# Half-column units, SBUF products and one shared PSUM tile in a long-convolution and gated-MLP kernel

## The chip, the cores and the metric

The kernel runs on one core of a Trainium2 chip. The metric is the device time of one execution in microseconds. Its engines are TensorE (PE, with its weight loads as PEld), VectorE (DVE), ScalarE (ACT), GpSimd (POOL, which here also issues the DMAs that store to scratch) and SyncE (SP, which issues all other DMAs). Matmul results land in PSUM, eight banks of 512 fp32 values in each of 128 partitions.

## The reference

With S = 2048 tokens, D = 640 columns, F = 1728 hidden units:

```python
xn = layernorm(A_q)                                   # no gain, no bias
k_shift = sum_t k[t - i] * shift_k[:, i], i = 0..3     # causal, four taps, by column
kv = k_shift * v
y = causal_conv(kv, ssm_k) + kv * ssm_D               # length S, by column (FFT of length 2S)
s = xn * y
g = silu(gelu_tanh(xn @ w1 + b1) @ w2 + b2)
out = A_q + s * g
```

All inputs and the output are bf16.

## The kernel before

The tokens lie as 128 partitions by 16 tiles `j` of 640 columns, so that the long convolution can be done as a transform of two steps with 64 x 32 points. D is added to the first tap of the kernel (`dadd`), so it needs no work of its own.

The work has these parts:
- **LN**: `stats`, `veps`, `pow` (POOL) and `xn`, for tiles in groups.
- **MLP**, in four chunks of four tiles: transposed `xn` (on PE for chunk 0, by DMA for the others), first layer `f1` (five matmuls of 512 columns for each of 14 hidden blocks, then a gelu on ACT), second layer `f2` (14 matmuls of 320 columns for each tile and column half, then silu). Chunks 2 and 3 go through `f1_wide`, which takes both into one two-bank tile and one gelu of 1024.
- **kv**: the four taps on DVE, six instructions per pair of tiles (L518 to L525).
- **Stage 1** (`s1_unit`, for the kernel `k` and for `u` = kv): for each tile two column halves, two matmuls each (L497), an eviction cast to SBUF on ACT or DVE (L234) and one store of 320 KB to scratch in DRAM (`scrK`, `scrU`; POOL, L501). The scratch turns partitions into the second transform's rows.
- **Convolution**, eleven units of three rows by 640 columns. A unit loads `kin` and `uin` (L586, SP), does stage 2 on PE (L596: eight matmuls side by side on 64 x 32 tiles of the array, four such packs a unit), casts the k result (L234), multiplies the u result straight from PSUM with it on DVE (L617, twice, 1920 products each: real and imaginary parts of one with both of the other), sums the four products in the first inverse step I1 on PE (L629, 32 matmuls, two of its four rounds with a third table), casts that (L234) and stores it to `scrC` (POOL, L638). It needs all 16 tiles of stage 1 for both k and u, with all columns.
- **End**: `cin` loads `scrC` (L644), I2 (L652) is the second inverse step, `ym` (L656, DVE) multiplies it from PSUM into `xn`, `f2m` (L470) does so with the MLP's result, `fin` (L448) adds x, and `store` (L450) writes the tile.

PSUM is four tiles of two banks. `G`, the second inverse table, is `W` transposed by 16 matmuls (L354) and one copy.

The order of all work is written out by hand: `ORDER` names for each operation its engine and its buffers, and `plan.emit` issues them in this order. Each engine, and each engine's DMA queue, works in order.

Of the kernel before, what the change touches and what calls it, by code (L numbers as in the profile page):

```python
# [32 lines left out]
NU = (NK1 + UK - 1) // UK  # L33
# [3 lines left out]
class Buf:  # L37
    def __init__(self, v=None, pool=None, parts=0):
        self.v, self.pool = v, pool
# [11 lines left out]
class Pool:  # L51
    def __init__(self, views, after=(), name=""):
        self.views, self.after, self.name = list(views), list(after), name
# [4 lines left out]
class Plan:  # L58
# [36 lines left out]
    def emit(self):  # L95
        seen = set()
        for i, e, slots in self.order:
            o = self.ops[i]
            assert o not in seen and all(d in seen for d in o.deps) and all(d in seen for d in o.after)
            for b, s in zip(o.allocs, slots):  # L100
                b.v = b.pool.views[s]
            o.fn(e)
            seen.add(o)
        assert len(seen) == len(self.ops)
# [13 lines left out]
1g 1g -2d 24d -6s 7d 1d -13s -1s -5a 13s -10s 17a 38d -54s 8s -4s 35d 1d -23a -20d -5g 30s 111p00 -112d -3p1 16d 7d  # L118
97p21 -10p32 -95d 9g 97a -104d 105p2 -137s 131d -5a -86d -23g 103p33 -70d -55g 143a -86d 70p2 -106a -14s 31g 88a 2a
-120s 4s 27d 19d 74p0 -86d -6d -6s 13p10 4p3 82a -85a 11d 1g -11p2 4p0 1d 7d -36s 39d -12a -2a 157d -70p1 -68p30 2p  # L120
2p2 2p 133d -115p0 116d -71a -49p1 -17a 62g 76d -178s 59p -29d 8a 11p3 -5a -13d 148d -128p -50s 61a -20a 3p2 -82d 217d
-133p 13a 3p 34g -45a 6a -8a -56s 197d 1d -146a 147d -145a 16a 130d -141p1 65p32 -11g 88d -76d -86s1 163d -162s 86p2
-66a 153d -171s 19p -20s 78p03 -57a 65a -140s 133a 201p3 -107d -86g -7p1 94d -93a 86p20 -207s 117g 92p0 -1a 7d 106p
-251p11 140a 6d -142p2 248a0 -169p02 75d -157a 84p3 -83p 82d -32g -46p 80a -83a 250d -246a 140d 12d -18g -136a 148p01
1d 1p3 -139p1 92s 40p03 2p2 6a -69g 62d 2a -133p 139g -79p30 2p0 -68p2 140g -135a -3p 5a 54p12 8a -150s 229d -81a -4p0
-62a 11p3 2p 247d -199a 87d -79g -24p11 18d -61a 10a 2a 244d -212a 211d -207p03 209d -252p2 44a -4p3 17g -12p1 -4a
-39p 44d 208d -158p00 -108p3 -91s 245d -141a -11p 108p1 -1a -94a -14a 165d -112g 70p02 -121a 123p2 -67g 42s 157p3
-147a 16a 28d 112g -182p11 40a 144d -182p2 -196a 276d 1d -108p03 26a 2a 180d -156g 147p -9p1 -189a 1p2 66g 143d
-191p00 180a1 -91d 108d -1d -352s 355d -9d -19p -188a 98p32 -80a 89d -81g 73a 116d -196p2 198d -46p0 -151a 80p3 19d
-256s 138g 107d 90d -105p21 116s0 -188g 99d 69a0 -88a 20d 89s -115p1 95d -88g 20d -260s 234a 76p 11p3 -69p13 -20a  # L130
15p20 109g -45a1 -63a 1p0 -282d 283a 72p -61d -26g -47p22 169d -103p0 -1a 76p1 31d -11s -26a0 -72g -61p3 72d 96d -103a
13p01 -79a 81p2 89d -29p 31s1 -88d -17g 18d -5a 6d -4a -80a -21p00 142d -36d -104p2 105d 1d 35p3 -41g -99a -2a 21g
-27p23 124d -122p0 147p -148a 8g 116d 72s -83p21 84s -39d -156a 163a1 -162g 112p0 10d -11a 2a 23p1 -42p22 87s 14s
-49a0 -32g 9d 24d -52a 29d -28p0 19p30 22p -20p2 -1a 9d 131s0 -159a 29p33 -28g 20d 10p0 3p21 7a0 -5p1 -14g 8a 2a 3d
64p310 -62a 124p02 -46p1 -82g 67a 16a -78g 85p3 2p1 38a 9s1 -46a 34s0 -55p2 19a 38d 2p0 1d0 1p1 -53p3 8p0 46d1 -61a
67s1 -59a 8a 52p23 2d -8p10 9p3 -7a 5d -6a 16s2 -6p2 -62p0 61d2 -60a 62d0 6s2 1p13 -6p20 7a 1d 1p1 -8a -73p3 74d 9p2
-81p0 80d1 7s0 -88a 83d0 -127d 133s3 1p13 12s4 -10d -1a -17g -77p2 104s1 -8p1 -91a 82p30 -86a 117s1 -21d2 1p2 1d0 -11a
18p31 -17a 20p0 -1a -8p12 7a -95p3 98d1 -8a -89a 98p2 -47g 53s2 -16d 18p01 11s0 -136p3 127a -9d0 -9g 28s0 -11a 2p1
21s1 -148a 118p20 2a 9p3 -10a 9d2 21s3 -12p01 2a -138p2 137a -8d0 10p1 -9p30 -129a 131a -1a -11g 41s4 -133p2 66g 46d1
1p0 8p13 -7d0 -113p 121d 1a -121a1 2p3 111p01 9p2 1d2 -122d 129s2 13s0 -29a -205d 194g 12a -112p 3p0 -2a1 120p1 8p23  # L140
2a -127p 118d0 8a -125a0 127p3 -9p12 -104p0 106a 9p2 -1d1 -9a 18p31 -140d 141a -123p 121s2 4p3 8s1 -18d0 9a -123a1
# [8 lines left out]
def kernel(  # L150
# [35 lines left out]
    smi = sb.tile([P, 256], F32, name="smi")  # L186
    pcol = sb.tile([P, 8], F32, name="pcol")
    pint = sb.tile([P, 8], I32, name="pint")
    tabs = sb.tile([P, 256], BF16, name="tabs")
# [5 lines left out]
    mv = sb.tile([P, NJ, nc.vector.BN_AGGR_DIM], F32, name="mv")  # L195
    veps = sb.tile([P, NJ], F32, name="veps")
# [6 lines left out]
    xnT = sb.tile([P, 2, DT, CH * P], BF16, name="xnT")  # L203
    hT = sb.tile([P, 2, FT, CH * P], BF16, name="hT")
    kT = sb.tile([P, NJ, D], BF16, name="kT")
    k_all = sb.tile([P, NJ + 3, D], BF16, name="k_all")
    v_all = sb.tile([P, NJ, D], BF16, name="v_all")
# [4 lines left out]
    def flat(t):  # L212
        return t[:].rearrange("p a d -> p (a d)")

    wb = mm[:, 0:4 * D].rearrange("p (a d) -> p a d", d=D)
    kt_t = mm[:, 4 * D:8 * D].rearrange("p (a b d) -> p a b d", a=2, d=D)
    kt_a = mm[:, 8 * D:10 * D].rearrange("p (a d) -> p a d", d=D)
    stg_t = [mm[:, (10 + 2 * i) * D:(12 + 2 * i) * D].rearrange("p (a d) -> p a d", d=D) for i in range(4)]
# [491 lines left out]
```

## Time and profile before

| | us |
|---|---|
| median of 3 runs (lowest to highest) | 216.5 (215.83 to 217.42) |
| profiled execution | 216.13 |
| its span, first to last instruction | 214.4 |
| PE, DVE, ACT busy | 179.4, 166.2, 126.5 |
| mean granted TensorE clock | 0.967 |

Busy time of an engine is the union of its instructions. The span leaves out the 1.73 us around the first and the last instruction. The first matmul of the MLP stands at 19.4 us, the first of the convolution at 102, and the last I1 ends at 180.6.

### The profile page before, as it was taken

Reading aid. Unit: us, or ns where it says so; the run is one execution under the profiler, and the core shown is the slowest. Engines: PE = TensorE matmul, PEld = TensorE weight load, DVE = VectorE, ACT = ScalarE, POOL = GpSimd, SP = SyncE. Lnnn points to the kernel's source line nnn. Section 1 sums busy time; section 2 is a strip of 40 time slices with the busy share of each in tenths; the row PEclk is TensorE's granted clock in tenths of the full one; section 3 lists DMA queues with packets and bytes.
Section 4 is the critical chain, followed back from the end, with each engine's and each line's share of the span. In section 5 each row is a group of like instructions: output and inputs, shape, how many; then the busy total and the mean of one; then the engine's idle time right before and its main releaser. Section 6 shows DMA issues by size and latency. Waiting matters only on the chain.

```text
span 214.4 us, 4137 instructions
## 1 busy us (share of the span) xinstructions
PE 179.4 (84%) x1660; PEld 90.4 (42%) x1660; DVE 166.2 (78%) x233; ACT 126.5 (59%) x163; POOL 37.6 (18%) x62
## 2 busy tenths in 40 slices
PE   0448999979988999998999899698999968999810
PEld 0314443633335665564443333233565523666500
DVE  6997998959889999964218997967756887029994
ACT  5298455877788977589554555868765764111100
POOL 7055000402252252324000020012100121100000
PEclk9999999999999999999999999999999995999985
DMA  5999998994379988949681749187980515599555
GB/s 165 373 418 412 413 356 203 361 387 172 144 214 369 242 247 206 255 151 343 214 276 27 250 144 303 27 272 257 292 278 6 199 49 192 160 415 409 207 199 198
DMA packets 28021, 52.54 MB, mean 245 GB/s; under 512 B 10081, under 2 KB 20834, under 8 KB 27874
## 3 DMA queue, kind: packets, MB, share of 16 engines
q1 hardware_dynamic: 23952, 35.89, 51.6%
q0 software_dynamic: 3904, 16.39, 20.3%
q8 instruction: 13, 0.21, 0.4%
q14 instruction: 6, 0.05, 0.1%
q10 hardware_dynamic: 146, 0.00, 0.0%
HBM read 31.95 MB, written 18.35 MB: 235 GB/s over the span
## 4 chain that ended last, share of the span: by engine, by line
PE 58%; DVE 20%; DMA 11%; issue 5%; ACT 3%; POOL 0%; DVEq 0%; ACTq 0%; POOLq 0%
PE ps L465 24%; PE ps L431 14%; PE ps L416 10%; DMA scrK<-mm 7%; DVE xn L656 5%; DVE k_all L617 5%; PE ps L629 4%; PE ps L596 3%; PE ps L497 3%; DMA x<-in_x_dram 2%; DVE stats L370 2%; DVE x L448 2%; DMA b_r<-in_b_dram 1%; DVE kT L448 1%; DVE mm L234 1%
## 5 line engine op out<-in xcount | busy, mean ns | idle before, releaser
L465 PE MATMUL ps<-w_sb,hT 128*128 128x320 bf16 x448 | 66.5, 303 | 1.4 <-ACT hT L420 0.8
L617 DVE TENSOR_TENSOR k_all<-ps,k_all 128x1920 bf16<-128x1920 f32 (+1 forms) x22 | 45.5, 2093 | 20.1 <-PE ps L596 17.1
L465 PEld LDWEIGHTS <-hT 128*128 128x128 bf16 x448 | 42.4, 99 | 24.5 <-issue 8.4
L234 ACT CAST mm<-ps 128x640 bf16<-128x640 f32 x55 | 35.1, 699 | 12.6 <-PE ps L497 6.9
L416 PE MATMUL ps<-xnT,w_sb 128*128 128x512 bf16 (+1 forms) x140 | 34.0, 393 | 1.9 <-ACT hT L420 1.6
L431 PE MATMUL ps<-xnT,w_sb 128*128 128x512 bf16 (+1 forms) x140 | 32.2, 380 | 0.6 <-ACT hT L439 0.5
L420 ACT ACTIVATE hT<-ps,b_f 128x512 bf16<-128x512 f32 (+1 forms) x28 | 18.2, 685 | 11.0 <-PE ps L416 11.0
L469 ACT ACTIVATE sl<-ps 128x640 bf16<-128x640 f32 x16 | 11.3, 707 | 21.5 <-PE ps L465 13.7
L439 ACT ACTIVATE hT<-ps,b_f 128x1024 bf16<-128x1024 f32 (+1 forms) x14 | 15.5, 1112 | 13.2 <-PE ps L431 13.1
L234 ACT CAST v_all<-ps 128x960 bf16<-128x960 f32 (+1 forms) x19 | 17.2, 947 | 9.0 <-PE ps L629 9.0
L416 PEld LDWEIGHTS <-w_sb 128*128 128x128 bf16 (+1 forms) x140 | 13.3, 101 | 20.0 <-issue 7.5
L638 POOL DMA_DIRECT2D scrC<-v_all x11 | 8.2, 749 | 73.0 <-ACT v_all L234 33.7
L431 PEld LDWEIGHTS <-w_sb 128*128 128x128 bf16 (+1 forms) x140 | 13.0, 98 | 18.0 <-issue 4.4
L234 ACT CAST k_all<-ps 128x960 bf16<-128x960 f32 (+1 forms) x16 | 14.2, 927 | 5.1 <-PE ps L596 4.1
L497 PE MATMUL ps<-kT,W 64*128 64x320 bf16 x64 | 8.9, 337 | 9.3 <-DMA kT<-in_kT_dram 8.3
L629 PE MATMUL ps<-k_all,tabs 32*64 32x480 bf16 (+1 forms) x352 | 13.3, 397 | 3.7 <-DVE k_all L617 1.9
L501 POOL DMA_DIRECT2D scrK<-mm x16 | 8.8, 550 | 42.8 <-ACT mm L234 35.3
L470 DVE TENSOR_TENSOR xn<-xn,sl 128x640 bf16<-128x640 bf16 x16 | 7.6, 484 | 9.9 <-ACT sl L469 9.9
L497 PEld LDWEIGHTS <-W 64*128 64x128 bf16 x128 | 4.8, 95 | 20.7 <-issue 11.6
L656 DVE TENSOR_TENSOR xn<-ps,xn 128x640 bf16<-128x640 f32 x16 | 12.6, 816 | 1.1 <-PE ps L652 1.1
L501 POOL DMA_DIRECT2D scrU<-mm x16 | 8.9, 556 | 19.0 <-ACT mm L234 14.7
L521 DVE TENSOR_TENSOR mm<-k_all,mm 128x2560 bf16<-128x2560 bf16 x8 | 11.9, 1490 | 0.2
(75 smaller groups left out, 176.7 us busy)
## 6 DMA issues: line engine op xcount, KB each, us to landing
scrK<-mm POOLq DMA_DIRECT2D x16, 320.0 KB, 6.6
scrU<-mm POOLq DMA_DIRECT2D x16, 320.0 KB, 3.3
k_all<-scrK SPq DMA_DIRECT2D x10, 480.0 KB, 3.9
v_all<-scrU SPq DMA_DIRECT2D x10, 480.0 KB, 4.7
scrC<-v_all POOLq DMA_DIRECT2D x10, 480.0 KB, 3.7
mm<-scrC SPq DMA_DIRECT2D x6, 640.0 KB, 6.4
kT<-in_kT_dram SPq DMA_DIRECT2D x4, 640.0 KB, 8.8
v_all<-in_v_dram SPq DMA_DIRECT2D x4, 640.0 KB, 7.1
```

Source lines behind the costliest of these rows:

```text
L234: (nc.scalar.copy if e == "ACT" else nc.vector.tensor_copy)(out=out_, in_=in_)
L416: nc.tensor.matmul(out=ps.v[0:M, i, :], lhsT=w1_sb[:, ft, t, 0:M], rhs=xnT_b[c].v[:, t, :], start=(t == 0), stop=(t == DT - 1))
L420: op("gelu", "ACT", lambda e, i=i, ft=ft, M=M: nc.scalar.activation(out=hT_b[c].v[0:M, ft, :], in_=ps.v[0:M, i, :], func=ACT.Gelu_apprx_ta ...
L431: nc.tensor.matmul(out=ps.v[0:M, i, :], lhsT=w1_sb[:, ft, t, 0:M], rhs=xnT_b[c + i].v[:, t, :], start=(t == 0), stop=(t == DT - 1))
L439: nc.scalar.activation(out=o, in_=s, func=ACT.Gelu_apprx_tanh, bias=b1_f[0:M, ft:ft + 1], scale=1.0)
L465: nc.tensor.matmul(out=ps.v[:, h, 0:H], lhsT=hT_b[c].v[0:M, ft, q * P:(q + 1) * P], rhs=w2_sb[0:M, ft, h * H:(h + 1) * H], start=(ft == 0) ...
L497: nc.tensor.matmul(out=ps.v[:, h, 0:H], lhsT=W[r, j, :], rhs=src[r, j, cs], start=True, stop=True)
L501: op("s1st" + kind, "POOL", lambda e: nc.gpsimd.dma_start(out=by_k1(scr)[:, 2 * j:2 * j + 2, :], in_=o.v), reads=[o], writes=[scr_b[j]], s ...
L521: op("kv2", "DVE", lambda e: tt(out=kt_t, in0=win(2, 2), in1=wbc(2, 2), op=ALU.mult), reads=kb + [wb_b], writes=[kvt_b])
L617: op("prod", "DVE", lambda e, ps=ps, qb=qb, kin=kin, w=w: nc.vector.tensor_tensor(out=qb.v[:, 0:4 * w].rearrange("p (i r w) -> p i r w", i ...
L629: nc.tensor.matmul(out=pc[g // 2].v[64 * r:64 * r + 64, g % 2, 0:w], lhsT=I1[tb][32 * g:32 * g + 32, :], rhs=qs[qi].v[32 * g:32 * g + 32, ...
L656: op("ym", "DVE", lambda e, j=j, ps=ps: nc.vector.tensor_tensor(out=hv(xn[:, j, :]), in0=ps.v[:, :, 0:H], in1=hv(xn[:, j, :]), op=ALU.mult ...
```

## The change

It does the following, with a new `ORDER` for all of it:
- k, v, the kernel and the three scratch arrays are laid out as two **column halves** `b` of 320. Stage 1 of u, kv and the convolution run by half; a kv step takes four tiles of one half, with the same instruction sizes as before. A store carries 160 KB in rows of 640 B; stage 1 of k makes two per tile.
- A convolution unit has six rows of one half (six units a half, the last of two rows) and is worked in **half units of three rows**. Stage 2 writes both parts of a half unit into one pair of banks, in two packs of eight matmuls of 240 columns (L638).
- Both the k and the **u result are cast** to SBUF (L259). The products are taken there in bf16, two instructions of 960 a half unit (L651), and **combined on DVE** into real and imaginary part, two instructions of 480 (L658, L659).
- **I1** (L669) then has two rounds instead of four: 16 matmuls a unit.
- `inv_unit` does I2 and `ym` for two tiles of one half (L691, L698), so a tile's `fin` waits for both halves and the MLP.
- PSUM is **one tile of eight banks**, given out by bank (`f1`, `f2`, `xt`) or by pair. `f1_wide` is gone; each gelu takes 512 and each silu 320 columns.
- `G` comes from four DMA transposes on SP (L386). Ten matmuls on zeros (`warm`, L300) are added. One tile's statistics are taken on ACT (L400). POOL may do `f2m` and `fin`. The small tables are built with fewer instructions.

```diff
-    ps_t = [psum.tile([P, 2, 512], F32, name="ps%d" % i) for i in range(4)]
+    ps_t = psum.tile([P, 8, 512], F32, name="ps")
...
-    op("gtr", "PE", gtr, reads=[W_b, id_b], writes=[ps])
...
+    for i in range(CH):
+        op("gtr", "SP", lambda e, i=i: nc.sync.dma_start_transpose(
+            out=G[:, 4 * i:4 * i + 4, :], in_=W[:, 4 * i:4 * i + 4, :].rearrange("p a b -> p (a b)")), reads=[W_b], mods=[G_b],
+           size=128 * 1024)
...
+        for t in range(nh):
+            for nm, src in (("s2k", kin), ("s2u", uin)):
+                ps = pair()
+
+                def s2(e, src=src, ps=ps, t=t):
+                    for i in range(2):
+                        for r in range(2):
+                            for g in range(4):
+                                nc.tensor.matmul(out=ps.v[32 * g:32 * g + 32, r, i * w:(i + 1) * w],
+                                                 lhsT=F2[i][64 * r:64 * r + 64, :],
+                                                 rhs=part(src.v[64 * r:64 * r + 64], t)[:, g * w:(g + 1) * w], start=True, stop=True)
+
+                chain("s2", op(nm, "PE", s2, reads=[src[t], tab_b], writes=[ps], extra=last("s2")))
+                op("s2ev", "ACT|DVE", lambda e, src=src, ps=ps, t=t: evict(
+                    e, part(src.v, t).rearrange("p (r c) -> p r c", r=2), ps.v[:, :, 0:2 * w]), reads=[ps], writes=[src[t]],
+                   size=4 * w)
+
+            def prod(e, t=t):
+                q = qb.v[:, t * 8 * w:(t + 1) * 8 * w].rearrange("p (r i m c) -> p r i m c", r=2, i=2, m=2)
+                ku, uu = (part(x.v, t).rearrange("p (r i c) -> p r i c", r=2, i=2) for x in (kin, uin))
+                for r in range(2):
+                    nc.vector.tensor_tensor(out=q[:, r], in0=uu[:, r, :, None, :].to_broadcast([P, 2, 2, w]),
+                                            in1=ku[:, r, None, :, :].to_broadcast([P, 2, 2, w]), op=ALU.mult)
...
+            def comb(e, t=t):
+                q = qb.v[:, t * 8 * w:(t + 1) * 8 * w].rearrange("p (r i m c) -> p r i m c", r=2, i=2, m=2)
+                nc.vector.tensor_tensor(out=q[:, :, 0, 0], in0=q[:, :, 0, 0], in1=q[:, :, 1, 1], op=ALU.subtract)
+                nc.vector.tensor_tensor(out=q[:, :, 1, 0], in0=q[:, :, 1, 0], in1=q[:, :, 0, 1], op=ALU.add)
...
+            for i in range(2):
+                for r in range(2):
+                    for g in range(4):
+                        nc.tensor.matmul(out=pc[g // 2].v[64 * r:64 * r + 64, g % 2, 0:nh * w].rearrange("p (t c) -> p t c", t=nh),
+                                         lhsT=I1[i][32 * g:32 * g + 32, :], rhs=q[32 * g:32 * g + 32, :, r, i, 0, :],
+                                         start=(i == 0), stop=(i == 1))
...
+    for b in range(2):
+        for u in range(NU):
+            conv_unit(b, u)
```

Three places of the order. On **DVE** where the products begin, the queue before has all kv steps (`mm`, `v_all`) behind it, then casts (L234) and products (L617):

```order
L523 TENSOR_TENSOR mm<-mm 128x1280
L525 TENSOR_TENSOR v_all<-mm,v_all 128x1280
L234 CAST mm<-ps_99 128x2x320 x2
L234 CAST k_all<-ps_97 128x960
L617 TENSOR_TENSOR k_all<-ps_97,k_all 128x1920
L617 TENSOR_TENSOR k_all<-ps_98,k_all 128x1920
L234 CAST k_all<-ps_100 128x960
```

In the changed kernel the first unit's products (L651) and combinations stand between a kv step of half 1 (L554), the normalization of later tiles (L425) and the statistics of the last ones (L415):

```order
L554 TENSOR_TENSOR mm<-mm 128x1280
L425 TENSOR_SCALAR xn<-kT,mv,rstd 128x640 x2
L497 TENSOR_TENSOR xn<-xn,sl_97 128x640
L651 TENSOR_TENSOR k_all<-v_all,xtra 128x960 x2
L658 TENSOR_TENSOR k_all<-k_all 128x2x240
L659 TENSOR_TENSOR k_all<-k_all 128x2x240
L651 TENSOR_TENSOR k_all<-v_all,xtra 128x960 x2
L658 TENSOR_TENSOR k_all<-k_all 128x2x240
L659 TENSOR_TENSOR k_all<-k_all 128x2x240
L415 BN_STATS stats<-kT 128x6 x2
```

The products have moved ahead of two kv instructions, two statistics, five normalizations and the second half's last stage-1 casts.

On **DVE** at the end, the queue before alternates `ym` (L656) and `fin` (L448) to the last row:

```order
L656 TENSOR_TENSOR xn<-ps_99,xn 128x640
L470 TENSOR_TENSOR xn<-xn,sl_95 128x640
L448 TENSOR_TENSOR kT<-xn,kT 128x640 x3
L448 TENSOR_TENSOR x_85<-xn,x_85 128x640 x2
L656 TENSOR_TENSOR xn<-ps_98,xn 128x640
L448 TENSOR_TENSOR x_85<-xn,x_85 128x640
L656 TENSOR_TENSOR xn<-ps_100,xn 128x640
L448 TENSOR_TENSOR x_85<-xn,x_85 128x640
```

In the changed kernel the eight `ym` of half 0 (L698) follow the last cast of the convolution, and the queue ends with the MLP's product (L497) and `fin` (L473):

```order
L473 TENSOR_TENSOR x_86<-xn,x_86 128x640
L497 TENSOR_TENSOR xn<-xn,sl_97 128x640
L473 TENSOR_TENSOR kT<-xn,kT 128x640 x2
L698 TENSOR_TENSOR xn<-ps,xn 128x2x320
L473 TENSOR_TENSOR kT<-xn,kT 128x640
L497 TENSOR_TENSOR xn<-xn,sl_98 128x640
L473 TENSOR_TENSOR kT<-xn,kT 128x640
```

What comes last has moved from I2 and `ym` to the second layer of the MLP.

On **SP** where the convolution's loads begin, the queue before holds only loads of `scrK` and `scrU` (L586), after all transposes of `xn`:

```order
L586 DMA k_all<-scrK 128x3x640 x2
L586 DMA v_all<-scrU 128x3x640
L586 DMA k_all<-scrK 128x3x640
L586 DMA v_all<-scrU 128x3x640 x2
L586 DMA k_all<-scrK 128x3x640 x2
```

In the changed kernel the loads (L621) alternate with the transposes of `G` (L386) and of the third and fourth chunk's `xn` (L450):

```order
L386 DMA_TRANSPOSE G<-W 128x4x128
L621 DMA k_all<-scrK 128x6x320
L621 DMA v_all<-scrU 128x6x320
L450 DMA_TRANSPOSE xnT<-xn 128x5x128
L386 DMA_TRANSPOSE G<-W 128x4x128
L621 DMA k_all<-scrK 128x6x320
L621 DMA v_all<-scrU 128x6x320
L450 DMA_TRANSPOSE xnT<-xn 128x5x128 x2
L621 DMA xtra<-scrK 128x6x320
```

The second unit's loads have moved behind one transpose of `xn` and one of `G`.

On PE the new order, counted in matmuls, is: first layer of chunk 0 (70, with stage 1 between), second layer of chunk 0 (112), first layer of chunk 1 (70), the first stage-2 operation (16), second layer of chunk 1, in which the first I1 stands behind four of its eight groups, and from there chunks 2 and 3 with the rest of the convolution between them. Behind the last I1 stand 140 matmuls of the second layer and 64 of I2; before there were 112 and 64.

More of the change, by code (lines that the diff above doesn't have):

```diff
@@ L100, in emit @@
             for b, s in zip(o.allocs, slots):
[L101 removed]
+                b.v = b.pool.view(s, b.width)
             o.fn(e)
@@ L202 @@
     w2_sb = sb.tile([P, FT, D], BF16, name="w2_sb")
[L203 to L207, printed above, removed]
+    xnT = sb.tile([P, 2, DT, CH * P], BF16)
+    hT = sb.tile([P, 2, FT, CH * P], BF16)
+    kT = sb.tile([P, 2, NJ, H], BF16, name="kT")
+    k_all = sb.tile([P, 2, NJ + 3, H], BF16, name="k_all")
@@ L263 @@
     op("first", "DVE", c0, writes=[bias_b, mh_b])
+    op("zero", "DVE", lambda e: nc.vector.memset(xtra[:, 0:D], 0.0), writes=[z_b])
+    for _ in range(10):
+        ps = bank()
+        op("warm", "PE", lambda e, ps=ps: nc.tensor.matmul(out=ps.v[:], lhsT=xtra[:, 0:P], rhs=xtra[:, P:P + 512], start=True, stop=True),
+           reads=[z_b], writes=[ps])
     def iotas(e):
@@ new lines, in conv_unit, with inv_unit, mmy, ym @@
+            op("i1ev", "ACT|DVE", back, reads=[pc[i]], mods=[uin], size=2 * nh * w)
+        op("cst", "POOL", lambda e: nc.gpsimd.dma_start(out=by_n2(scrC)[:, b, k0:k1, :],
+                                                        in_=uin.v[:, 0:n].rearrange("p (k d) -> p k d", d=H)),
+           reads=[uin], writes=[scrC_b[b][u]], size=P * n * 2)
+    def inv_unit(b, i, cb):
+        j = 2 * i
+        ps = pair()
+        def mmy(e):
+            for t in range(2):
+                for h in range(2):
+                    nc.tensor.matmul(out=ps.v[64 * h:64 * h + 64, t, 0:H], lhsT=G[:, j + t, 64 * h:64 * h + 64],
+                                     rhs=cb.v[:, h, j % 4 + t, :], start=True, stop=True)
+        op("i2", "PE", mmy, reads=[cb, G_b], writes=[ps])
+        def ym(e):
+            xv = xn[:, j:j + 2, b * H:(b + 1) * H]
+            nc.vector.tensor_tensor(out=xv, in0=ps.v[:, :, 0:H], in1=xv, op=ALU.mult)
+        op("ym", "DVE", ym, reads=[ps], mods=[xn_b[j], xn_b[j + 1]])
+        step_done(j)
+        step_done(j + 1)
```

508 lines of the change are left out of this document (245 added, 263 removed).

## The prediction

> **What bounds the kernel now.** First the window view, cut at four points of the chain: the first matmul of the MLP (19.4), the first matmul of the convolution (102), the end of its last I1 (180.6), the end. Above it the sums of the page's first part.
>
> ```profile
> PE 179.4 (84%) x1660; PEld 90.4 (42%) x1660; DVE 166.2 (78%) x233; ACT 126.5 (59%) x163; POOL 37.6 (18%) x62
> ```
>
> ```profile
> core 0: us, PE busy (x) PEld busy (x) DVE busy (x) ACT busy (x) POOL busy (x), PEclk, DMA share, GB/s
> 0.00:19.40 19.40, 7.41 (x52) 4.53 (x53) 16.04 (x43) 11.81 (x14) 8.99 (x19) 1.00 0.89 335
> 19.40:102.00 82.60, 78.40 (x494) 38.97 (x502) 72.18 (x118) 61.45 (x92) 20.34 (x33) 1.00 0.85 275
> 102.00:180.60 78.60, 71.05 (x947) 32.56 (x948) 56.67 (x36) 49.69 (x53) 6.97 (x10) 0.97 0.57 186
> 180.60:214.40 33.80, 22.56 (x176) 14.39 (x176) 21.34 (x37) 3.50 (x5) 1.26 (x2) 0.85 0.69 258
> ```
>
> In the second stage PE is busy 95% and DVE 87%; in the third PE 90% (71.05 of 78.6), DVE 72%, ACT 63%; in the last nobody is full, because it is a sequence: the scratch round trip, then DVE. Each stage follows the other, and DVE's slack lies in the third and the last. The chain that ended last shows the same and gives what PE work costs in a row:
>
> ```profile
> 19.43 15.99 PE ps L416 x65
> ...
> 69.67 2.06 PE ps L465 x14
> 71.73 0.38 PE ps L497 x4
> 72.11 2.01 PE ps L465 x14
> ...
> 101.98 0.53 PE ps L596 x16
> 102.52 8.96 PE ps L431 x40
> ...
> 123.72 1.02 PE ps L629 x32
> 124.74 0.33 PE ps L596 x8
> ...
> 180.58 10.86 PE ps L465 x70
> 191.44 0.41 PE ps L652 x4
> ...
> 211.09 0.49 DVE x L448
> ```
>
> So an MLP matmul of 512 columns costs 0.224 us (8.96/40), a second-layer group of 14 costs 2.01, four stage-1 matmuls 0.38. Stage 2 comes in packs of eight that run side by side: sixteen take 0.53, eight 0.33, so a pack of 480 columns is 0.20 and the rest, about 0.13 to 0.2, is paid per excursion. An I1 of 32 is four packs, 0.95 to 1.02. After the last I1, at 180.58, come 33.8 us: PE fills 10.86 with second-layer groups while scrC is written and read, then DVE alone works from 191.9 to 211.6, then the last store takes 2.8 (214.4 less 211.58).
>
> **The change, part by part.** The durations:
>
> ```profile
> L617 DVE TENSOR_TENSOR k_all<-ps,k_all 128x1920 bf16<-128x1920 f32 x20 | 42.6, 2154 | 19.6 <-PE ps L596 17.1 <-issue 1.3 <-ACT v_all L234 0.7
> L234 ACT CAST v_all<-ps 128x960 bf16<-128x960 f32 x18 | 16.5, 961 | 8.5 <-PE ps L629 8.5
> L521 DVE TENSOR_TENSOR mm<-k_all,mm 128x2560 bf16<-128x2560 bf16 x8 | 11.9, 1490 | 0.2
> L469 ACT ACTIVATE sl<-ps 128x640 bf16<-128x640 f32 x16 | 11.3, 707 | 21.5 <-PE ps L465 13.7 <-DVE xn L656 6.3 <-DVE xn L470 1.3
> L470 DVE TENSOR_TENSOR xn<-xn,sl 128x640 bf16<-128x640 bf16 x16 | 7.6, 484 | 9.9 <-ACT sl L469 9.9
> L234 DVE CAST mm<-ps 128x640 bf16<-128x640 f32 x9 | 7.4, 824 | 5.7 <-PE ps L497 3.0 <-DMA scrK<-mm 2.3 <-issue 0.5
> L234 DVE CAST k_all<-ps 128x960 bf16<-128x960 f32 x6 | 6.8, 1152 | 3.2 <-PE ps L596 2.2 <-issue 1.0
> L656 DVE TENSOR_TENSOR xn<-ps,xn 128x640 bf16<-128x640 f32 x16 | 12.6, 816 | 1.1 <-PE ps L652 1.1
> L420 ACT ACTIVATE hT<-ps,b_f 128x512 bf16<-128x512 f32 x26 | 17.0, 686 | 11.0 <-PE ps L416 11.0
> L439 ACT ACTIVATE hT<-ps,b_f 128x1024 bf16<-128x1024 f32 x13 | 14.5, 1112 | 10.8 <-PE ps L431 10.6
> ```
>
> *Products (DVE).* Removed: 22 products straight from PSUM, 45.6 us (42.6 and two shorter ones). Added: 40 products of 960 elements and 4 of 640, and 40 combinations of 480 and 4 of 320, all in SBUF. Between the rows of 640 (484 ns) and 2560 (1490) an SBUF product costs 0.524 ns an element and 149 fixed. Hence 652 for 960, 484 for 640, 400 for 480, 317 for 320: 28.0 + 17.3 = 45.3. The products move no DVE time; twice the rate is spent on the combinations. No row shows a product whose both inputs repeat along a middle dimension; L521 has one such input. The bounds are 652 ns and one element per PSUM rate, (2154 - 154)/1920 = 1.04 ns, that is 1.15 us; I take 652, the nearest shape.
>
> *Evictions.* The u results, until now read from PSUM by the product, must now be cast: 22 more of about 960 elements. By the new order DVE makes 20 conv casts (16 of 960, 2 of 640, 2 of 320: 21.1 us by 1152, 824 and an estimate of 0.49, 824 less 320 at 1.04) instead of 9 (10.0), ACT 48 (44.5 us by 961) instead of 35 (31.4). DVE also makes 3 more stage-1 casts (+2.5) and gives POOL four 640-element operations (-1.9). So DVE goes from 166 to about 177 us in sum and ACT, with unpaired gelus (56 x 0.686 = 38.4 against 17.0 + 14.5 and 2.5 for the last, shorter ones) and halved silus (32 x 0.44, an estimate: 707 less 320 x 0.83, the slope between L420 and L439), from 126 to about 146.
>
> *PE.* I1 halves: ten of two packs (0.53) and two short ones (0.27) are 5.8 us against 10.5, a gain of 4.7. The sixteen transposes of W leave PE (1.9). Stage 2 has twice the matmuls at half the columns: 44 operations of two packs of 240. Between a pack cost proportional to its columns (0.10) and one that stays at 0.20 lie 8.8 us; I take 0.10, since the start of a matmul on another tile of the array costs next to nothing in these rows:
>
> ```profile
> L596 PE MATMUL ps<-v_all,tabs 64*32 64x320 bf16 x16 | 0.7, 305 | 0.5 <-ACT k_all L234 0.3 <-ACT v_all L234 0.2
> 174.87 0.33 PE L596 MATMUL ps<-v_all,tabs 64*32 64x320 bf16 x8 [0.22 <-ACT v_all L234]
> ```
>
> Eight matmuls of 305 ns each are over in 0.33 us, so seven starts lie within 25 ns, some 4 ns apart.
> The Trainium skill, "TensorE: Matmul & The Clock Gate", section "Wait — 56ns, not 53.3ns?", says instead that start-to-start never drops below about 25 ns however few columns there are. By that rule sixteen matmuls need 0.40 us whatever their width, stage 2 costs 8.8 us more, and that is the fourth rival below. The trace speaks against it for matmuls on different tiles of the array, and the same page's section "The mechanism" also gives about 4 ns there.
>
> *Scratch and queues.* The rows of scrK, scrU and scrC become 640 B instead of 1280 to 2560, and POOL issues 64 stage-1 stores of 160 KB instead of 32 of 320. The bytes are the same; DMA is at 0.57 in the third stage. POOL, 37.6 us busy, has room for some 20 us of issues. What counts is the latency:
>
> ```profile
> scrU<-mm POOLq DMA_DIRECT2D x16, 320.0 KB, 3.3
> k_all<-scrK SPq DMA_DIRECT2D x10, 480.0 KB, 3.9
> v_all<-scrU SPq DMA_DIRECT2D x10, 480.0 KB, 4.7
> scrC<-v_all POOLq DMA_DIRECT2D x10, 480.0 KB, 3.7
> mm<-scrC SPq DMA_DIRECT2D x6, 640.0 KB, 6.4
> ```
>
> The four transposes of G move to SP, where two stand ahead of the second unit's loads; until 94 us DVE has no room for that unit, so that is the cover. Ten warming matmuls lie in PE's idle time before 19.4, two between stage-1 groups (0.2 each).
>
> *When the convolution begins.* Half 0 needs only the first half's u. In PE's new queue 140 first-layer matmuls (31.4), ten second-layer groups (20.1), 88 stage-1 matmuls (22 x 0.38 = 8.4) and one stage-2 operation stand ahead of the first s2u: 60 us after 19.4, that is 80, against 102 now with all u behind it. The last u store and its reload (0.7 + 0.6 + 3.3 + 4.7 after the last stage-1 group of half 0, ten us of PE work earlier at 70) land at 80 as well. But DVE is later. To 102 us it now spends 16.04 + 72.18 = 88.2 us; of that the new order puts behind the first product two kv steps, two statistics, five normalizations, two casts and one MLP product, and ACT takes one statistic: about 9 us. That leaves 79. With 16 of it done at 19.4, and 90% busy after (87% now), the first product starts at 19.4 + 63/0.9 = 90, and the first unit's combinations end at 94.3 (4.2 us of DVE). PE's I1 of that unit stands behind two second-layer groups, so PE arrives at about 85.5 and waits nine us: everything queued behind it, the next s2 and the MLP, waits too.
>
> *From there to the last I1.* DVE has left: 20 half units of 2.1 us (40.8 with the two short ones), casts 21.0, stage-1 casts 4.1, two statistics 2.3, five normalizations 2.2, five MLP products 2.4, kv 1.6: 74.4, less about 3.4 for consecutive operations that overlap (the x16 of L656 fill 12.6, not 13.1): 71. PE has 140 first-layer matmuls 31.4, ten groups 20.1, sixteen stage-1 matmuls 1.5, 40 stage-2 operations 8.0 and 17 excursions 3.4, I1 5.8: 70.2. ACT has about 75 from 77 on. The two bounds are equal; the present third stage ran its one bound engine at 90%, so with two I take 87%: 71/0.87 = 81.6, and the last I1 ends at 176 instead of 180.6.
>
> *The tail.* Behind it PE has ten second-layer groups, 20.1, and sixteen I2 (0.27 for four matmuls plus 0.14 a switch from the 0.41 row, seven switches), 5.3: 25.4. Half 1's first I2 stands 10.4 us down that queue; cast, store and reload (0.5 + 0.8 + 3.2 + 6.4) take 10.9, so 0.5 to 0.7 of waiting. DVE's rest is sixteen L656 (12.6), fourteen final adds and four MLP products (18 x 0.42), 20 us, and lies beside PE's 25.4, because half 0's eight are done before half 1 arrives. Then silu 0.44, product 0.48, add 0.48, gaps 0.15, store 2.8: 4.35. Together 30.4 against 33.8.
>
> **The sum.** 176 + 30.4 = 206.4 us of span, 8 less than 214.4. The profiled execution took 216.13, 1.73 more than its span, and 0.4 less than the median of 216.5. So 208.1, rounded **208**: 3.9% faster. The gain is two parts of about 4: the stages overlap, and the DVE-only tail becomes a PE tail.
>
> **Rivals.**
> 1. *The queues feed each other better*: DVE is busy 95% of the stretch, near what it reaches now in the middle of the second stage:
>
> ```profile
> 60.00:90.00 30.00, 28.62 (x212) 16.69 (x210) 29.32 (x48) 23.33 (x36) 10.82 (x15) 1.00 0.93 263
> ```
>
>    Last I1 at 169, time 201. Against it: PE must then be busy 94% too.
> 2. *In-order waits eat the gain.* Each of the twelve I1 waits in PE's queue for combinations that wait for casts that wait for that PE. L617 idled 17.1 us for L596 in this way. A loss of 0.9 us a unit more than I took (77% busy) puts the last I1 at 186.5 and the time at 219. From 0.7 us a unit the gain is gone.
> 3. *Slower: SBUF products at one element per cycle.* Place: L651 and its two combinations. Price 0.52 ns on 61,400 elements, 32 us, all on the engine that bounds: 100 us at 92% after a first unit of 7, last I1 at 206, time 238. It decides from 0.83 us a product of 960 (8 us over 44). For it: two repeated inputs and strides that no row shows; against it: L521.
> 4. *A half-length pack costs a full one*: 8 us more on PE after the first I1; 78.2 at 90% is 87 us, last I1 at 181.5, time 214. It is the mechanism to which the 25 ns rule would lead.
>
> **Chances.** Forecast 0.50 (203 to 213), first rival 0.13, second 0.20 (215 to 223), third 0.07, fourth 0.10. To leave out two in ten at most, the range runs from 199 to 219: it takes in the forecast, the first, the fourth and about half of the second. Less than 1% is about what a measurement of this kernel tells from no change. Faster by more: 0.48 + 0.13 + half of the fourth, 0.66; within: 0.02 + 0.08 + 0.05 = 0.15; slower: 0.12 + 0.07 = 0.19.
>
> **What would show it.** L651 at 0.65 us and L658 at 0.40 (third rival: 1.15). First L651 at about 90, and a PE wait of several us at the first L669. Sixteen L638 matmuls in about 0.3 to 0.4 us (fourth: 0.53). DVE busy near 177, ACT near 146. Last I1 at 176, and from there PE, not DVE, on the chain to within 5 us of the end. I am wrong if the first product waits for scrU beyond 95, if DVE is under 80% busy from 94 to the last I1, or if half 1's I2 waits for its reload more than 2 us.

## The result

| | before | changed |
|---|---|---|
| median, lowest to highest | 216.45 us (215.83 to 217.42, 4 runs) | 205.25 us (203.5 to 209.48, 4 runs) |
| profiled execution, its span | 216.13, 214.4 | 204.61, 202.4 |
| PE, DVE, ACT busy | 179.4, 166.2, 126.5 | 175.4, 172.3, 138.4 |

The ratio is **0.945** (95% interval 0.937 to 0.953), faster by 5.5%. The forecast was 208 in a range of 199 to 219. Executions of the changed kernel scatter more than those of before; ratios, and the means given below, leave out executions that ran markedly slower than the fastest ones of the same kernel, so they can differ from the medians.

The windows of the changed kernel, cut at the first matmul of the MLP, the first I1, the end of the last I1 and the end. The columns are as in the prediction. The first I1 is not the event at which the kernel before was cut: 102 was its first matmul of stage 2, and its first I1 stood at 116.9. Here the first matmul of stage 2 stands at 86.4; the last two rows are cut there.

```profile
0.00:19.40 19.40, 7.97 (x39) 3.52 (x40) 14.37 (x39) 9.39 (x13) 8.10 (x24) 1.00 0.92 337
19.40:97.90 78.50, 69.98 (x486) 33.73 (x485) 69.07 (x107) 58.07 (x94) 38.91 (x54) 1.00 0.91 280
97.90:173.00 75.10, 72.59 (x1131) 35.05 (x1130) 67.77 (x123) 64.22 (x88) 18.38 (x23) 0.98 0.89 249
173.00:202.40 29.40, 24.88 (x211) 16.18 (x204) 21.10 (x35) 6.67 (x13) 5.20 (x4) 0.99 0.64 202
19.40:86.40 67.00, 58.86 (x342) 27.16 (x339) 59.40 (x84) 46.88 (x77) 34.05 (x47) 1.00 0.89 288
86.40:173.00 86.60, 83.71 (x1266) 41.63 (x1266) 77.45 (x144) 75.41 (x105) 23.24 (x30) 0.98 0.91 246
```

The difference between length and PE's busy time is PE's idle time. Before it was 12.0, 4.2, 7.6 and 11.2 us in the four stages, 35.0 in all; now, with stage 2 as the cut in both, it is 11.4, 8.1, 2.9 and 4.5, together 27.0. The 12 us of span that went are thus **8 us of PE idle time and 4 us of PE's busy time** (179.4 to 175.4, although 4.9 of warming matmuls are new). The idle time went in the tail (-6.7) and in the convolution (-4.7). The second stage has 3.9 more, although it is 16 us shorter.

The convolution's end and the tail, from the chain that ended last:

```profile
172.75 0.28 PE ps L669 x16
173.02 2.01 PE ps L491 x14
175.03 0.94 PE ps L691 x12
...
193.96 3.93 PE ps L491 x28
197.93 0.04 issue
197.98 0.45 ACT sl L495
198.45 0.50 DVE xn L497
198.97 0.49 DVE kT L473
```

From 173 to 197.9 the chain is PE alone (and from 115 on with but 3 us of ACT between); before, DVE followed DVE from 191.9 on. And the groups that answer to those of before:

```profile
L651 DVE TENSOR_TENSOR k_all<-v_all,xtra 128x960 bf16<-128x960 bf16 x16 | 9.7, 652 | 0.3
L659 DVE TENSOR_TENSOR kT<-kT 128x480 bf16<-128x480 bf16 x8 | 3.2, 399 | 0.0
L669 PE MATMUL ps<-k_all,tabs 32*64 32x480 bf16 (+1 forms) x128 | 4.4, 339 | 0.0
L669 PE MATMUL ps<-kT,tabs 32*64 32x480 bf16 x64 | 2.8, 421 | 0.0
```

I1 never waits (idle before it 0.0); its sum is 7.2 us.

### The profile page after: what moved, and what is told of

It reads as the page before. It is cut to its first block, busy times and chain, and to the rows that moved or that the text cites. A ratio compares the mean times of both kernels' runs of the same rounds, so it can differ in the third digit from the quotient of the medians.

```text
span 202.4 us, 4736 instructions
## 1 busy us (share of the span) xinstructions
PE 175.4 (87%) x1846; PEld 88.5 (44%) x1846; DVE 172.3 (85%) x301; ACT 138.4 (68%) x206; POOL 70.6 (35%) x103
## 4 chain that ended last, share of the span: by engine, by line
PE 47%; issue 17%; DMA 13%; POOL 13%; DVE 5%; ACT 3%; SPq 1%; POOLq 0%; ACTq 0%; DVEq 0%
PE ps L459 18%; PE ps L491 18%; DMA scrU<-mm 9%; POOL scrK L532 6%; POOL scrU L532 4%; PE ps L638 4%; DMA x<-in_x_dram 3%; PE ps L669 3%; PE ps L691 3%; ACT mm L259 2%; POOL rstd L422 2%; DVE mm L259 1%; DVE stats L415 1%; PE ps L524 1%; ACT L495 1%
## 5 line engine op out<-in xcount | busy, mean ns | idle before, releaser
L459 PE MATMUL ps<-xnT,w_sb 128*128 128x512 bf16 (+1 forms) x280 | 68.9, 392 | 4.7 <-ACT mm L259 3.5
L259 ACT CAST mm<-ps 128x640 bf16<-128x640 f32 x52 | 34.2, 698 | 23.1 <-PE ps L524 11.2
L459 PEld LDWEIGHTS <-w_sb 128*128 128x128 bf16 (+1 forms) x280 | 25.6, 100 | 41.5 <-issue 17.1
L463 ACT ACTIVATE hT<-ps,b_f 128x512 bf16<-128x512 f32 (+1 forms) x56 | 36.7, 697 | 8.1 <-PE ps L459 8.0
L532 POOL DMA_DIRECT2D scrU<-mm x32 | 22.3, 753 | 42.7 <-ACT mm L259 37.5
L259 ACT CAST v_all<-ps 128x960 bf16<-128x960 f32 (+2 forms) x34 | 30.3, 928 | 3.8 <-PE ps L669 2.3
L495 ACT ACTIVATE sl<-ps 128x320 bf16<-128x320 f32 x32 | 14.1, 445 | 21.5 <-PE ps L491 21.2
L532 POOL DMA_DIRECT2D scrK<-mm x32 | 23.4, 903 | 5.7 <-ACT mm L259 5.3
L524 PEld LDWEIGHTS <-W 64*128 64x128 bf16 x128 | 5.3, 97 | 25.9 <-issue 19.4
L698 DVE TENSOR_TENSOR xn<-ps,xn 128x640 bf16<-128x640 f32 x16 | 12.5, 816 | 4.1 <-PE ps L691 4.0
L259 DVE CAST v_all<-ps 128x960 bf16<-128x960 f32 (+2 forms) x12 | 12.2, 1014 | 4.3 <-PE ps L669 2.2
L259 DVE CAST mm<-ps 128x640 bf16<-128x640 f32 x12 | 9.6, 817 | 6.8 <-PE ps L524 5.9
L553 DVE TENSOR_TENSOR mm<-k_all,mm 128x2560 bf16<-128x2560 bf16 x8 | 11.9, 1485 | 0.2
L550 DVE TENSOR_TENSOR mm<-k_all,mm 128x2560 bf16<-128x2560 bf16 x8 | 11.9, 1486 | 0.1
L638 PEld LDWEIGHTS <-tabs 64*32 64x32 bf16 x704 | 7.6, 90 | 9.5 <-issue 8.4
L651 DVE TENSOR_TENSOR k_all<-v_all,xtra 128x960 bf16<-128x960 bf16 x16 | 9.7, 652 | 0.3
L651 DVE TENSOR_TENSOR kT<-v_all,k_all 128x960 bf16<-128x960 bf16 x16 | 9.6, 650 | 0.1
```

What stands on the lines that cost most here:

```text
L259: (nc.scalar.copy if e == "ACT" else nc.vector.tensor_copy)(out=out_, in_=in_)
L459: nc.tensor.matmul(out=ps.v[0:M, :], lhsT=w1_sb[:, ft, t, 0:M], rhs=xnT_b[c].v[:, t, :], start=(t == 0), stop=(t == DT - 1))
L463: op("gelu", "ACT", lambda e: nc.scalar.activation(out=hT_b[c].v[0:M, ft, :], in_=ps.v[0:M, :], func=ACT.Gelu_apprx_tanh, bias=b1_f[0:M, f ...
L495: op("silu", "ACT", lambda e, h=h, ps=ps: nc.scalar.activation(out=sl.v[:, h * H:(h + 1) * H], in_=ps.v[:, 0:H], func=ACT.Silu), reads=[ps ...
L524: nc.tensor.matmul(out=ps.v[:, h, 0:H], lhsT=W[r, j, :], rhs=src[r, b, j, :], start=True, stop=True)
L532: nc.gpsimd.dma_start(out=by_h(scr)[:, b, :, j, :], in_=o.v[:, b])
```

## The experiments

**Which engine sets the convolution's stage?** Two kernels add TensorE work there, one takes VectorE work away.

```diff
-            for i in range(2):                  # i1
+            for i in (0, 1, 0, 1):              # e1;  (0, 1) * 4 in e9
```

> The changed kernel, but every I1 runs its two rounds twice into the same banks (16 more matmuls in each of 12 units, so the number of matmuls of before; the result is the same). That is 20 packs of 240 columns in two pieces and four short ones, +5.2 us of PE by 0.53 us for each ten-unit pair of packs, +5.8 by all. My theory (PE, busy 97% from the first to the last I1, now sets that stretch): the time rises by nearly all of it, +4 to +6 us, to about 209.5 against 204.6. Rival A (DVE sets it, PE has slack): +0 to +2 us.

> The changed kernel with every I1 run four times into the same banks (the result is the same): 12 units with 64 matmuls instead of 16. An I1 of 32 took 0.95 us where one of 16 takes 0.54, so this adds three times 5.0 us, 15 us of TensorE between the first and the last I1. Doubling alone moved the time by only about 2 of its 5 us. If TensorE sets the stretch once its idle 2.5 us and the like are used up, +10 to +15 us over the changed kernel's 203.4 (the mean of its six undisturbed runs so far), 214 to 218. Rival A (something else sets it and TensorE's work is half hidden throughout): +4 to +7 us, about 209.

```diff
-                nc.vector.tensor_tensor(out=q[:, :, 0, 0], in0=q[:, :, 0, 0], in1=q[:, :, 1, 1], op=ALU.subtract)
-                nc.vector.tensor_tensor(out=q[:, :, 1, 0], in0=q[:, :, 1, 0], in1=q[:, :, 0, 1], op=ALU.add)
```

> The changed kernel without the two combinations of each half unit (L658, L659); it leaves that part of the computation out, I1 takes the uncombined products. DVE loses 44 x 0.40 = 17 us. My theory (PE sets the stretch): 0 to -2.5 us, about 203 against 204.6, since PE's idle time in it is 2.5 us in all. Rival A (DVE sets it): from -7 to -15 us, about 193.

Means: changed kernel 203.4 (six executions of two comparisons), I1 twice 205.3 (two), I1 four times 212.75 (two), without combinations 202.8 (three; median 203.22). The windows from the first to the last I1, of I1 four times and of the kernel without combinations:

```profile
97.20:183.87 86.67, 84.24 (x1707) 43.77 (x1706) 68.42 (x124) 65.23 (x89) 18.27 (x23) 1.00 0.82 218
```

```profile
96.60:170.85 74.25, 70.96 (x1131) 34.51 (x1130) 53.62 (x80) 64.56 (x88) 18.91 (x23) 1.00 0.94 253
```

Seventeen microseconds less VectorE work bought 0.6 us: DVE fell to 53.6 of 74.25 and the stage kept its length. Thirteen us more TensorE work by I1's rows (15 in the forecast) cost 9.3 us and PE stayed 97% busy. So PE sets this stage, as I expected; but the price is less than forecast. I1 twice adds 4 us by its rows (I1's sum goes from 7.2 to 11.2) and costs 1.9, where I expected 4 to 6; by itself it fell into rival A's range, and only the runs with four rounds and without combinations decide. I1 four times costs 0.7 of the added work, 9.3 us where I expected 10 to 15. The rest found room in 2.5 us of idle time and, in this profile, in the clock: at 1.00 instead of 0.98 the first layer (L459) takes 66.0 us, not 68.9. Two executions each are few for the exact slope.

**Are the shared banks what lets PE run at 97%?** The control gives the banks out by a rule; the variant uses the same rule and the same queues, but a one-bank operation occupies a pair.

```diff
-            for b, s in zip(o.allocs, slots):
-                b.v = b.pool.view(s, b.width)
+            if b.width == 2 or PAIRS:                   # PAIRS: False in e3, True in e4
+                c = [[s, s + 1] for s in range(0, 8, 2) if s not in live and s + 1 not in live]
+            else:
+                c = [[s] for s in range(8) if s not in live]
+            return min(c, key=lambda m: (max(free_at[s] for s in m), -free_at[m[0] ^ 1])) if c else None
```

> Control for the next one: the changed kernel with the same queues on every engine, but the PSUM banks are given out anew by a rule (the free bank, or pair, whose last reader stands earliest), not by the written table. Both theories: within 2 us of the changed kernel, since eight banks stay shared bank by bank.

> The same rule as the control, but every operation that needs one bank (f1, f2, transposes) occupies a pair, as in the kernel before: four pairs instead of eight banks. The order on each engine stays. My theory (the stretch runs at 97% instead of the 87% of my sum because the banks let PE run ahead of ACT and DVE): +6 to +12 us against the control, about 212, most of the difference between the two efficiencies of 75 us. Rival B (the efficiency comes from the order alone, with stage 2 placed units ahead): +0 to +2 us.

Control 203.86 us (203.48 to 204.29), ratio to before 0.947, within the 2 us expected; pairs **219.67** (217.66 to 227.23), ratio 1.017 (1.008 to 1.025). The loss is 16 us, beyond my 6 to 12, and the rest of the change together is then no gain at all. The stage from the first to the last I1 in the control and with pairs, and PE's longest MLP waits in the kernel with pairs (L520 is the first layer, L552 the second):

```profile
98.00:172.20 74.20, 71.22 (x1131) 34.95 (x1130) 68.10 (x123) 64.49 (x89) 18.88 (x23) 1.00 0.93 252
103.50:186.30 82.80, 71.49 (x1130) 35.72 (x1129) 68.29 (x122) 64.86 (x88) 18.94 (x23) 1.00 0.81 225
```

```profile
PE ps L520 <- ACT mm L320: 5.5, 5, 1.9
PE ps L552 <- DVE v_all L320: 4.7, 4, 1.9
```

With pairs MLP matmuls wait for casts of the convolution and of stage 1 that hold a pair; PE is busy 86% there, against 96% in the control. That is close to the 87% of my sum, which I had set a little under the 90% of the old stage with its four pairs. Of the 16 us this stage has 8.6; the first I1 comes 5.5 later, and the tail is 2.3 longer. It shows what one-bank operations gain from banks of their own under this order; an order written for pairs may lose less, but no run has one.

**Is the early start worth anything?**

```diff
+        conv = ("kin", "uin", "s2k", "s2u", "s2ev", "prod", "comb", "i1", "i1ev", "cst")
+        cut = max(n for n, (i, e, s) in enumerate(self.order) if self.ops[i].kind == "s1stu")
+        head, rest = self.order[:cut + 1], self.order[cut + 1:]
+        moved = [x for x in head if self.ops[x[0]].kind in conv]
+        self.order = [x for x in head if self.ops[x[0]].kind not in conv] + moved + rest
```

> The control with banks given by rule, but all 74 operations of the convolution that the written order places ahead of the last stage-1 store of u (five units' loads, 19 stage-2 operations, eight products and combinations, three I1) are moved behind it, in the same order among themselves: the convolution begins only when all u is stored, as in the kernel before. My theory (a part of the gain is that the convolution's VectorE work lies beside the MLP of the second stage): eight half units of products and combinations (17 us) and about nine casts (9 us) of DVE go behind 111 us, where DVE has some 7 us of idle time; +8 to +20 us, 212 to 224 against the control's 203.9. Rival C (the overlap of the stages buys nothing, the work of TensorE saved by the shorter I1 does): within 3 us of the control.

225.92 us (223.85 to 226.82), ratio 1.047 (1.040 to 1.053): 22 us lost, 2 more than the upper end of my 8 to 20. The first I1 stands at 122.2 instead of 97.9:

```profile
122.20:192.70 70.50, 57.11 (x1007) 27.32 (x1008) 57.59 (x104) 52.71 (x68) 9.08 (x11) 0.80 0.75 220
```

The stage is only 4.6 us shorter although it starts 24 later: it has 1007 matmuls instead of 1131, so a part of PE's work that would have filled it has been done before. PE idles 13.4 us in it and the granted clock is 0.80. This order was written for the early start, so the 22 us are the price of taking that start away from it, not the gain of the change.

**The arithmetic alone, in the kernel before.** First with the u cast queued at its product, then queued at its stage-2 matmuls.

```diff
+            us = us_t[i]                                   # e7: here;  e10: behind the matmuls of s2u
+            (nc.scalar.copy if i == 0 else nc.vector.tensor_copy)(out=us[:, :, 0:w], in_=ps.v[:, :, 0:w])
-                in0=ps.v[:, None, :, 0:w].to_broadcast([P, 2, 2, w]),
+                in0=us[:, None, :, 0:w].to_broadcast([P, 2, 2, w]),
+            if i == 1:                                     # two combinations of 2 * w, then I1 in two rounds
+                nc.vector.tensor_tensor(out=q0[:, 0:2 * w], in0=q0[:, 0:2 * w], in1=q1[:, 2 * w:4 * w], op=ALU.subtract)
+                nc.vector.tensor_tensor(out=q0[:, 2 * w:4 * w], in0=q0[:, 2 * w:4 * w], in1=q1[:, 0:2 * w], op=ALU.add)
```

> The kernel before with the new arithmetic alone: both u results of a unit are cast to SBUF (the first on ACT, the second on DVE), two products of 1920 elements in SBUF, two combinations of 960 on DVE, I1 with two rounds instead of four. Units, loads, stores, PSUM tiles and order stay. DVE per unit: 2 x 1.155 + 2 x 0.652 + 1.152 (one cast) = 4.77 against 4.31; ACT +0.96 a unit; PE -0.48 a unit, 5 us in all. My theory (the arithmetic alone is neutral, since the products wait for two steps more and every stage is still a sequence): 213 to 219, within 1.5% of before. Rival C (the PE work saved pays one for one): 210 to 211.5.

> The kernel before with the arithmetic alone once more, but each u cast is queued where its stage-2 matmuls stand, ahead of the casts of the unit before, instead of at the product. In the first form ACT's queue had the cast of a unit's u behind the last unit's I1 casts, and products idled 26.7 us for it. If the loss of 17 us was this place in ACT's queue: 214 to 219. Rival E (the units of three rows in four PSUM pairs leave no room for a longer chain cast, product, combination, I1, wherever the cast stands): 224 to 233.

232.62 us (ratio 1.078, 1.073 to 1.083) and 234.06 (1.083, 1.075 to 1.090). Both of my expectations for the first were wrong by over 13 us; for the second, rival E's range was missed by only 1 us. What PE waited for, in the kernel before and in the first variant (L638 is its I1, L627 the first combination):

```profile
PE ps L629 <- DVE k_all L617: 1.9, 3, 1.1
```

```profile
PE ps L638 <- DVE k_all L627: 11.3, 7, 2.4
```

And one round of it on the chain:

```profile
184.31 0.96 ACT v_all L235
185.28 0.87 ACT us L620
186.15 0.02 issue
186.17 1.16 DVE k_all L621
187.33 1.08 DVE us L620
188.41 0.02 issue
188.44 1.17 DVE k_all L621
```

A cast of the last unit's I1 (L235), a u cast, a product, a cast, a product, behind it the combinations: each waits for the one before, and only then comes the next I1. This is my second rival, the wait of one I1 for combinations that wait for casts; of the 17 us lost in the old kernel PE waits 11.3 for it. Moving the cast forward in the queue took PE's wait for the combinations from 11.3 to 6.3 us and the product's wait for the ACT cast from 26.7 to 12.9, and the time did not fall: PE's idle time from 117 to 197.5 us is 22.4 us in the first form and 21.4 in the second, with waits in other places. Now the u cast on DVE (L618) idles 20.3 us for stage 2.

```profile
PE ps L640 <- DVE k_all L629: 6.3, 5, 2.1
PE ps L597 <- ACT v_all L235: 2.3, 5, 0.8
PE ps L597 <- DVE v_all L235: 2.2, 1, 2.2
```

```profile
L618 DVE CAST us<-ps 128x960 bf16<-128x960 f32 (+1 forms) x11 | 12.4, 1126 | 20.3 <-PE ps L597 20.3
```

So it is not this one place in a queue. That the coarse units and the four pairs are to blame fits, but no run changed them in the old kernel alone.

**POOL's stores.** From 57.9 to 91.8 us the chain of the changed kernel runs mostly through store issues of stage 1 (L532) and the gaps between them. They are most of the rise of POOL from 37.6 to 70.6 us:

```profile
L532 POOL DMA_DIRECT2D scrK<-mm x32 | 23.4, 903 | 5.7 <-ACT mm L259 5.3
L532 POOL DMA_DIRECT2D scrU<-mm x32 | 22.3, 753 | 42.7 <-ACT mm L259 37.5
```

```diff
-                nc.gpsimd.dma_start(out=by_h(scr)[:, b, :, j, :], in_=o.v[:, b])
+                (nc.scalar if on[b - a] == "ACT" else nc.gpsimd).dma_start(out=by_h(scr)[:, b, :, j, :], in_=o.v[:, b])
```

> The changed kernel, but a stage-1 store whose half was cast by ACT is issued from ACT's queue instead of POOL's; the others stay on POOL. Theory D (the chain of waits from 60 to 92 us runs through POOL's store issues L532, and the staging buffers come free late): POOL loses some 30 us of busy time, the first I1 comes 2 to 4 us earlier than 97.9, and the time falls by 1 to 3 us. Rival (TensorE's own work sets the stage, or the issues cost ACT as much as they cost POOL): -0.5 to +2 us.

**220.1 us** (219.28 to 223.95, ratio 1.020), and the first I1 at 116.4 instead of 97.9: neither theory. POOL fell to 35.3 us busy, but 52 issues of 0.52 to 0.59 us (medians), some 30 us, went into ACT's queue, which had 20 us to spare in the second stage. The trace does not count them as busy:

```profile
19.40:97.90 78.50, 61.14 (x329) 27.65 (x325) 58.36 (x85) 45.43 (x72) 5.19 (x6) 0.89 0.74 235
```

```profile
32.69 0.52 ACTq L532 DMA_DIRECT2D scrU<-mm  x1
...
43.38 1.88 ACT L259 CAST mm<-ps 128x640 bf16<-128x640 f32 x3 [5.89 <-DMA scrU<-mm]
```

The second row shows the other half: a cast waits in ACT's queue until a store has landed and frees its staging buffer, and every gelu and every further store stands behind it. So whether POOL's issues bound the changed kernel stays open; that the kernel pays 16 us for having them in ACT's queue is shown.

**Two small parts.** Without the ten matmuls on zeros, and with POOL's gating products and adds on DVE:

```diff
-        op("warm", "PE", lambda e, ps=ps: nc.tensor.matmul(out=ps.v[:], lhsT=xtra[:, 0:P], rhs=xtra[:, P:P + 512], start=True, stop=True),
+        op("warm", "PE", lambda e: None,                # e11
...
+            if o.kind in ("f2m", "fin"):                # e12
+                e = "DVE"
             o.fn(e)
```

> The changed kernel without the ten matmuls on zeros (L300). Two lie between stage-1 groups after TensorE's start, the others in its idle time before 19.4 us. Both theories: within 1 us of the changed kernel; if their absence lowers the granted clock at the start, up to 2 us slower.

> The changed kernel with the gating products and final adds that POOL takes (L497 and L473, some 1.4 to 1.55 us each there) back on DVE at the same places of the order (0.48 us each). My theory (neither DVE nor POOL sets the time): -0.5 to +0.7 us. Theory D (POOL's queue of stores sets the second stage): -1 to -3 us.

204.86 us (ratio 0.947, 0.942 to 0.952) and 201.8 (0.935, 0.928 to 0.942). The changed kernel once more, in five rounds, gave 203.84:

> The changed kernel once more, in five rounds on the same chip as the next three, as their common measure. Both theories: 203.5 to 206 us. The profile of the first one lost some 2.9 us in the first layer (L459 68.9 us against 66.0 to 66.1 in two other profiles) in a stretch in which the granted clock fell; without such a stretch its span should be 200 to 201.

Its ratio there was 0.938 (0.932 to 0.943), against 0.945 at first. Neither small part can be told from it. The second one is the lowest median of all and lies in the range of theory D, not of mine, but its interval overlaps. What its trace shows is told in the last section.

## Why the prediction was right, point by point

- **Products and combinations**: 652 and 400 ns taken, 652 and 399 measured. The third rival (1.15 us) is out. That they move no DVE time held, with 44.2 us for the groups of L651, L658 and L659 against 45.6 removed. DVE's sum rose by 6 us (11 forecast), ACT's by 12 (20 forecast).
- **Stage 2 in packs of 240**: sixteen matmuls take 0.40 us, inside my 0.3 to 0.4, not 0.53; the fourth rival is out. In the longer excursions of the chain 48 take 0.74 us, 15 ns a matmul. By the Trainium skill's rule of about 25 ns from start to start ("TensorE: Matmul & The Clock Gate", "Wait — 56ns, not 53.3ns?") 48 matmuls would need 1.2 us, an estimate; the trace does not agree with it here.

```profile
125.77 0.74 PE ps L638 x48
```

- **When it begins**: wrong by 4 us for DVE and by 12 for PE. The first product stands at 93.63, not 90, and PE reached its first I1 at 97.9, not 85.5:

```profile
93.63 1.23 DVE L651 TENSOR_TENSOR k_all<-v_all,xtra 128x960 bf16<-128x960 bf16 x2
```

```profile
97.87 0.61 PE L669 MATMUL ps<-k_all,tabs 32*64 32x480 bf16 x16
```

  So the nine-us wait never came. The step that failed is "60 us after 19.4, that is 80": it gave PE no idle time, and PE has 8.5 us up to its first I1, mostly waiting for casts that free banks and for stage-1 inputs:

```profile
PE ps L459 <- ACT mm L259: 3.5, 3, 1.8
PE ps L524 <- ACT mm L259: 1.9, 4, 0.7
PE ps L524 <- DVE v_all L557: 1.5, 1, 1.5
```

  The other 4 us are work above the sum; the 140 first-layer matmuls, for one, took 34.0 us instead of 31.4. The reload of `scrU`, forecast to land at 80, was late too: it was issued at 87.4. DVE was late by less (64.9 us done by 93.6, 87% busy, where I took 63 at 90%), so PE and DVE met at the first unit. That PE did not have to wait there is luck, not foresight.

- **From the first to the last I1**: here the sum was mis-sized. I took 71 us of the busier engine at 87%, 81.6 us. Measured: 72.6 of PE at 97%, 75.1 us. That two bounds would hold each other up was wrong: DVE has 67.8 us there, and taking 17 us off it changes nothing. The 87% came from a stage with four PSUM pairs, to which the variant with pairs (86%) goes back. This is the first rival's "the queues feed each other better", but with PE at 97% as the full engine, not DVE, which is at 90%. A start 3.6 us later than forecast and a run 6.5 us shorter offset each other in part, by luck: last I1 at 173.0, 176 forecast.
- **The tail**: 29.4 us, 30.4 forecast, PE alone until 4.5 us before the end (4.35 forecast), and I2 never waits for its reload. This term, and its reason, held. Nor did any of the three signs of being wrong appear: DVE, for one, was 91% busy from 94 to the last I1.
- **The gain**: two parts of about 4 were named; the stages gave 7.6 (180.6 to 173.0) and the tail 4.4.

## What to carry to other kernels

Count PE's idle time by stage, before and after: it says where a gain came from when engines' sums hardly move. A share of busy time taken from an old stage holds only for the old buffers; when a change makes the buffers finer, ask what waits for a buffer, since here a pair where a bank would do cost more than the whole gain. And arithmetic that takes work from TensorE but lengthens the chain cast, product, combination cost 17 us in the old order: ask first what fills the wait.

## What the hardware showed unexpectedly

- **The granted clock was low in some stretches in which PE waited often.** In the kernel before with SBUF products (second form), from the first to near the last I1, PE was busy 73% and the clock 0.87; in the changed kernel, at 97%, it was 0.98:

```profile
117.00:197.50 80.50, 59.12 (x673) 26.12 (x666) 55.24 (x66) 50.59 (x57) 7.52 (x10) 0.87 0.47 150
```

  The Trainium skill, "TensorE: Matmul & The Clock Gate", section "HAM oscillation — how this bites in real kernels", gives as abstract rule that PE must have no idle gaps over about 3.4 us. No wait of that stretch reaches that: the longest of PE's waits there was 2.2 us (the rows of L640 and L597 above), but there were many. So staying under that figure did not keep the clock up here. The busy share alone does not decide either: with pairs, at 86% and with many waits, the clock was 1.00 (the row of 103.50:186.30 above). In the changed kernel one wait of 1.4 us at 113, with smaller ones around it, was followed by ten first-layer matmuls in 3.63 us that take 2.3 to 2.4 elsewhere:

```profile
114.39 0.40 PE L638 MATMUL ps<-k_all,tabs 64*32 64x240 bf16 x16 [1.43 <-DVE mm L259]
...
115.46 3.63 PE L459 MATMUL ps<-xnT,w_sb 128*128 128x512 bf16 x10
```

  From 116 to 120 us the granted clock was 0.57. Yet in the second profile of the same kernel the same wait, there of 1.58 us, was followed by ten such matmuls at the usual pace:

```profile
113.00 0.40 PE L638 MATMUL ps<-k_all,tabs 64*32 64x240 bf16 x16 [1.58 <-DVE mm L259]
...
114.06 2.33 PE L459 MATMUL ps<-xnT,w_sb 128*128 128x512 bf16 x10
```

  So one such wait sometimes costs twice and sometimes not. What decides it stays open: no run here varied the gaps alone.
- **An elementwise product on POOL takes three times as long**: 1.45 us for 640 bf16 elements against 0.48 on DVE.

```profile
L497 POOL TENSOR_TENSOR xn<-xn,sl 128x640 bf16<-128x640 bf16 x2 | 2.9, 1450 | 8.5 <-ACT sl L495 8.5
L497 DVE TENSOR_TENSOR xn<-xn,sl 128x640 bf16<-128x640 bf16 x14 | 6.8, 483 | 1.0 <-ACT sl L495 1.0
```

  It can also hold DVE up. The combination that DVE began during such a product took 1.52 us instead of 0.40 and ended 0.3 us after the product did; the cast behind it is the one for which PE waits 1.43 us above:

```profile
111.51 1.51 POOL L497 TENSOR_TENSOR xn<-xn,sl 128x640 bf16<-128x640 bf16 x1
111.77 1.52 DVE L658 TENSOR_TENSOR kT<-kT 128x480 bf16<-128x480 bf16 x1
```

  The second profile of the changed kernel and the control show it too (1.66 and 1.63 us). In the variant with these products on DVE the combinations there take 0.40 us, and PE has no gap from 108 to 118 us. Whether that is why this variant has the lowest median is not shown, since its interval overlaps.

- **A store's issue on POOL costs more for half the bytes**: 0.75 to 0.90 us for 160 KB in rows of 640 B (L532 above), where the kernel before needed 0.55 for 320 KB in rows of up to 2560 B:

```profile
L501 POOL DMA_DIRECT2D scrK<-mm x16 | 8.8, 550 | 42.8 <-ACT mm L234 35.3 <-ACT hT L420 5.3 <-DVE mm L522 2.2
```
